# One core, chunked linear attention and a SiLU MLP: weight pieces loaded ahead of token, value and block loads, unit 2's first keys earlier, unit 3's diagonal copied by VectorE

## The chip, the cores and the metric

The kernel runs on one NeuronCore of a Trainium2 chip. The core has five engines that run side by side, each in its own program order: TensorE (PE, with its weight loads shown as PEld), VectorE (DVE), ScalarE (ACT), GpSimd (POOL) and SyncE (SP). In this kernel nearly every DMA is issued by SP, so SP's program is one long queue of transfers, and a transfer starts only when SP has come to it. The metric is device time in microseconds (us), median of several runs. The profile shows one execution, and its times are counted from the start of its span.

## The reference: what is computed

Two blocks follow each other. The first is a linear attention with a state that decays per channel, over 4 batches, 8 heads, 768 tokens and 48 channels per head:

```python
for t in range(S):
    cur = einsum('bhd,bhe->bhde', u * k[t], v[t])
    y[:, :, t] = einsum('bhd,bhde->bhe', r[t], state + cur)
    state = w[t][..., None] * state + einsum('bhd,bhe->bhde', k[t], v[t])
```

Its output, as 3072 rows of 384, goes through an MLP: `h = x @ w_in` (384 to 2048), `g = h * sigmoid(h)`, `out = g @ w_out` (2048 to 384). The two weight matrices come in 64 bits, all else in 32.

## The kernel before, in words

**Units.** The tokens are cut into six chunks of 128, and the four batches into two pairs. That makes 12 units, numbered 0 to 11; a unit is 128 tokens of two batches and all heads. "Unit 2" below is the third.

**Attention of a unit.** Decays, queries and keys (w, r, k) are turned so that channels lie on partitions (`turn`, L360; for units from 2 on by VectorE transposes at L374, out of a room `raw` that two units use in turn). The scores of a chunk are built level by level, l = 0 to 6: at level l the queries (`grow_queries`, L624, VectorE) and the keys (`grow_keys`, L630, GpSimd) are multiplied with products of decays over 2^l tokens (`product`, L419, GpSimd), matmuls make scores (`score_products`, L688, matmul at L703), and VectorE (L721) or ScalarE (L800) keeps the wanted part of them in `score`. The first keys of unit 2 are made by `odd_ones` (L657, ScalarE) and `start_keys` (L662, GpSimd, tensor_tensor at L669); `level(2, 1)` (L757) is the first to use them. The diagonal of the scores has a path of its own: products on GpSimd (`bonus`, L434, lines 448, 450 and 452), sums on VectorE (L457, L461), four small DMAs (L467) that move the sums to where tokens lie on partitions, small copies (`bonus_spread`, L581, copies at L595 and L597), and a predicated copy into `score` (`bonus_write`, L604). From unit 4 on the diagonal goes by blocks of 8 tokens instead (`block_bonus`, `block_sum`, `block_move`, `block_spread`).

**From attention to MLP.** `y_state` and `y_values` (L834, L858) make the output yt of a unit, `update` (L884) the state. `move_x` (L920) moves yt into xt with ten DMAs on SP (L928). `up(i, m)` (L995, matmul at L1000) makes one eighth of the 2048 channels: twelve matmul records, six for each half, which read xt's three column groups c = 0, 1, 2 in this order. Its result lies in one of two PSUM rooms `p_h`, which ScalarE's SiLU (L1009) frees. `down` (L1017, L1022) is the second product for unit 0; from unit 1 on it is made of seven smaller products (`quarter`, L1052, L1066), which need sums of activations (`sums`, L1042) and of weights (`weight_sums`, L1038).

**Weights.** They come as 16 pieces, 0 to 15, of 768 KB each (8 of w_in, then 8 of w_out), by `load_weight` (L202, DMA at L206), and are made into 32-bit numbers by `head_weight` and `tail_weight` (ScalarE, L223, L225, L231), `join_weight` (VectorE, L242, L243) and `add_weight` (GpSimd, L255). A piece waits for room: pieces 11 to 15 may be loaded when pieces 5, 8, 9, 10 and 11 are joined, and `join_weight` issues those loads at its end.

**Order.** No scheduler orders the work: each call appends its instructions to the engines' programs, so the order of calls in `do(...)` is the order in each engine's queue. The first part, up to unit 2, is written out by hand (L1107 to L1163): lists `others[m]` stand between the weight pieces, and lists of block loads (`block_loads`, L949: sixteen DMAs of `load_blocks`, L114 and L123, for each of w, k and r of a unit) are dealt out among them. From unit 3 on a loop (L1165) lays each unit's groups from `mix(i)` (L954 on) between the steps of the MLP: the seven quarters of unit i-2, then the eight ups of unit i-1. In `mix`, the line `loads = ...` (L981) says which block loads a unit issues, and these are dealt out over its later groups. `move_x(3)` is in the second group of `mix(4)`, so on SP it stands behind all loads that `mix(3)` issues; `up(3, 0)` needs it. `move_x(2)` stands in the hand-written part, and `up(2, 0)` needs it.

## Time and profile before

| | |
|---|---|
| median of 3 runs | 598.62 us (598.1 to 599.99) |
| the profiled execution | 599.11 us, of which its span is 597.3 us |
| TensorE busy, matmuls | 587.5 us, 98% of the span |
| VectorE, ScalarE, GpSimd busy | 411.6, 232.7, 351.5 us |
| granted TensorE clock | 1.00 |
| chain that ended last | PE 82%, DVE 5%, POOL 4%, ACT 2%, SP's queue 2%, DMA 2% |

How to read it: busy time of an engine is the union of its instructions. A line of the timeline gives start and duration in us, engine (SPq is SP issuing a DMA), the line of the kernel, the operation, what is written and read, a count of merged instructions, and in brackets the idle time before it with what ended it. A DMA line of SP is the time of issuing it; its landing comes later (median 1.9 us for the xt transfers, 2.2 us for 32 KB of w, 6.4 us for a 768 KB piece of w_out, by the page's DMA part).

### The profile page before, as it was taken

Reading aid. Unit: us, or ns where it says so; the run is one execution under the profiler, and the core shown is the slowest. Engines: PE = TensorE matmul, PEld = TensorE weight load, DVE = VectorE, ACT = ScalarE, POOL = GpSimd, SP = SyncE. Lnnn points to the kernel's source line nnn. Section 1 sums busy time; section 2 is a strip of 40 time slices with the busy share of each in tenths; the row PEclk is TensorE's granted clock in tenths of the full one; section 3 lists DMA queues with packets and bytes.
Section 4 is the critical chain, followed back from the end, with each engine's and each line's share of the span. In section 5 each row is a group of like instructions: output and inputs, shape, how many; then the busy total and the mean of one; then the engine's idle time right before and its main releaser. Section 6 shows DMA issues by size and latency. Waiting matters only on the chain.

```text
span 597.3 us, 14760 instructions
## 1 busy us (share of the span) xinstructions
PE 587.5 (98%) x5790; PEld 527.8 (88%) x5790; DVE 411.6 (69%) x709; ACT 232.7 (39%) x516; POOL 351.5 (59%) x414
## 2 busy tenths in 40 slices
PE   8999999999999999999999999999999999999997
PEld 7787866699899899899899899889889889889997
DVE  7879788798596695596696696686587587542041
ACT  6788874531530540440350351361351251250110
POOL 5998768447578568278378477477477567500000
PEclk9999999999999999999999999999999999999999
DMA  9965794443542543543543643643543531101000
GB/s 227 301 148 149 157 283 75 59 76 51 126 61 66 106 66 52 129 69 53 130 67 55 138 62 52 130 65 52 120 75 52 113 63 27 36 1 28 28 0 27
DMA packets 203078, 53.42 MB, mean 89 GB/s; under 512 B 186752, under 2 KB 194816, under 8 KB 203008
## 3 DMA queue, kind: packets, MB, share of 16 engines
q1 hardware_dynamic: 201424, 51.88, 42.7%
q8 instruction: 46, 0.75, 0.6%
q10 hardware_dynamic: 1584, 0.59, 0.5%
q14 instruction: 24, 0.20, 0.1%
HBM read 43.21 MB, written 5.24 MB: 81 GB/s over the span
## 4 chain that ended last, share of the span: by engine, by line
PE 82%; DVE 5%; POOL 4%; ACT 2%; SPq 2%; DMA 2%; issue 2%; POOLq 0%; DVEq 0%; ACTq 0%
PE p_h L1000 35%; PE p_o L1066 34%; PE p_m L1022 3%; PE p_m L864 2%; PE p_sc L703 2%; PE p_m L843 2%; SPq L123 2%; PE p_m L703 1%; DVE score L721 1%; POOL w_out_sb L255 1%; PE p_sc L892 1%; PE p_sc L819 1%; DMA own<-in_moe_w_out_dram 1%; DMA raw<-in_r_dram 1%; DVE score L604 1%
## 5 line engine op out<-in xcount | busy, mean ns | idle before, releaser
L1000 PE MATMUL p_h<-xt,w_in_sb 128*128 128x256 f32 x1152 | 259.8, 383 | 1.6 <-POOL tk L669 0.7
L1000 PEld LDWEIGHTS p_h<-xt,w_in_sb 128*128 128x128 f32 x1152 | 215.5, 190 | 33.3 <-ACT gt L1009 1.3
L1009 ACT ACTIVATE gt<-p_h 128x512 f32<-128x512 f32 x90 | 53.5, 595 | 172.5 <-PE p_h L1000 172.2
L645 POOL TENSOR_TENSOR tk<-tk,tw 128x256 f32<-128x256 f32 x128 | 93.9, 755 | 35.4 <-issue 21.0
L507 POOL TENSOR_TENSOR ruk<-tokens_rk 128x768 f32<-128x768 f32 (+1 forms) x32 | 51.4, 1616 | 64.4 <-DMA tokens_rk<-in_k_dram 34.6
L1066 PE MATMUL p_o<-own,temps 128*128 128x192 f32 x528 | 87.9, 326 | 0.0
L1066 PE MATMUL p_o<-w_out_sb,gt 128*128 128x192 f32 x508 | 86.4, 326 | 0.0
L1066 PEld LDWEIGHTS p_o<-own,temps 128*128 128x128 f32 x528 | 86.1, 190 | 0.1
L1066 PEld LDWEIGHTS p_o<-w_out_sb,gt 128*128 128x128 f32 x508 | 83.4, 190 | 0.6
L1048 DVE TENSOR_TENSOR temps<-gt 128x256 f32<-128x256 f32 x84 | 50.3, 599 | 25.7 <-ACT gt L1009 25.3
L627 DVE TENSOR_TENSOR tr<-tr,tw 128x512 f32<-128x512 f32 x61 | 54.1, 887 | 14.7 <-PE p_m L703 11.2
L422 POOL TENSOR_TENSOR tw<-tw 128x256 f32<-128x256 f32 (+6 forms) x83 | 40.4, 487 | 35.4 <-DVE tw L374 31.5
L615 ACT COPY tk<-tk 128x256 f32<-128x256 f32 x52 | 21.0, 403 | 102.6 <-POOL tk L645 80.1
L721 DVE COPY_PREDICATED score<-mask,p_sc 128x512 f32<-128x512 int8 x42 | 31.1, 796 | 3.2 <-PE p_sc L703 3.0
L1075 DVE TENSOR_TENSOR partial<-p_o,partial 128x192 f32<-128x192 f32 x33 | 11.7, 355 | 27.8 <-PE p_o L1066 27.8
L1066 PE MATMUL p_o<-w_out_sb,temps 128*128 128x192 f32 x176 | 30.4, 326 | 0.0
L1048 DVE TENSOR_TENSOR temps<-temps,gt 128x256 f32<-128x256 f32 x43 | 29.1, 677 | 1.5
L1075 DVE TENSOR_TENSOR temps<-p_o,partial 128x192 f32<-128x192 f32 x22 | 7.9, 358 | 31.5 <-PE p_o L1066 25.3
L541 DVE TENSOR_REDUCE block_sums<-ruk 128x4 f32<-128x192 f32 (+1 forms) x48 | 24.2, 545 | 7.1 <-POOL ruk L507 7.1
L1066 PEld LDWEIGHTS p_o<-w_out_sb,temps 128*128 128x128 f32 x176 | 28.9, 190 | 0.0
L869 ACT COPY yt<-p_m 48x512 f32<-48x512 f32 x40 | 23.2, 581 | 13.9 <-PE p_m L864 13.1
L703 PEld LDWEIGHTS p_sc<-tr,tk 48*64 48x64 f32 x960 | 17.3, 134 | 12.1 <-issue 7.7
(188 smaller groups left out, 814.2 us busy)
## 6 DMA issues: line engine op xcount, KB each, us to landing
w_out_sb<-in_moe_w_in_dram SPq DMA_DIRECT2D x6, 768.0 KB, 7.6
w_out_sb<-in_moe_w_out_dram SPq DMA_DIRECT2D x4, 768.0 KB, 6.4
own<-in_moe_w_out_dram SPq DMA_DIRECT2D x4, 768.0 KB, 6.1
tokens_rk<-in_r_dram SPq DMA_DIRECT2D x8, 384.0 KB, 4.5
tokens_rk<-in_k_dram SPq DMA_DIRECT2D x8, 384.0 KB, 5.4
tokens_w<-in_w_dram SPq DMA_DIRECT2D x8, 384.0 KB, 6.4
xt<-yt SPq DMA_DIRECT2D x60, 48.0 KB, 1.9
raw<-in_w_dram SPq DMA_DIRECT2D x80, 32.0 KB, 2.2
```

Of the source, the lines that this page charges most:

```text
L422: engine.tensor_tensor(out=up, in0=t[:, :, 0::2], in1=t[:, :, 1::2], op=ALU.mult)
L507: mul = lambda out, one, two: nc.gpsimd.tensor_tensor(out=out, in0=one, in1=two, op=ALU.mult)
L541: add = lambda out, have: nc.vector.tensor_reduce(out=out, in_=have, axis=mybir.AxisListType.X, op=ALU.add)
L627: nc.vector.tensor_tensor(out=odd, in0=odd, in1=tw[i][l][:, :, 0::2][:, :, :, None].to_broadcast([128, Q, L >> (l + 1), c]), op=ALU.mult)
L645: nc.gpsimd.tensor_tensor(out=out, in0=have, in1=odd_products(i, l, b, *blocks), op=ALU.mult)
L703: nc.tensor.matmul(to, lhsT=tk[i][rows, X[l % 2] + p, x * 64:(x + 1) * 64], rhs=have, start=True, stop=True)
L721: nc.vector.copy_predicated(out=dst, mask=masks[l][:, :, None].to_broadcast([128, NB, NP, ni, c]), data=sc[e].rearrange("p (b q) (i c) -> ...
L869: nc.scalar.copy(out=yt[i][PD * e:PD * e + D, x::2, :, :], in_=p_yt[i, e][PD * x:PD * x + D].rearrange("p (q b) t -> p q b t", b=NB))
L1000: nc.tensor.matmul(p_h[:, a, :], lhsT=w_in_sb[:, c, f * 128:(f + 1) * 128], rhs=xt[i][:, c, :], start=(c == 0), stop=(c == KC - 1))
L1009: nc.scalar.activation(out=gt[i, m], in_=p_h, func=AF.Silu)
L1048: nc.vector.tensor_tensor(out=out, in0=one, in1=two, op=op)
L1066: nc.tensor.matmul(p, lhsT=left(f), rhs=right[:, f, :], start=(f == 0), stop=(f == FH - 1))
```

## The change

It has four parts, all in the order of calls or in the engine of one step.

1. `bonus_spread` copies with VectorE instead of ScalarE for units above 2, that is for unit 3 alone.
2. In `mix`, the r blocks of unit i+1 are issued in unit i already for i = 3 (before: from i = 4 on). So r of unit 4 is issued in `mix(3)`; the hand-written part now loads only w and k of unit 4.
3. In the hand-written part, the r blocks of unit 2 go behind piece 11, the values of unit 2 and the tokens of unit 3 (`load_values(2)`, `load_rk(3)`) behind pieces 14 and 15, and the blocks of unit 3 one to two places later.
4. For unit 2, `odd_ones`, the first `start_keys` and the products are called earlier, `reverse_v(2)` and `weight_sums(0)` later.

```diff
@@ bonus_spread
-        nc.scalar.copy(out=both_b[:, 0], in_=diag[i][0])
+        copy = nc.vector.tensor_copy if i > NTOK else nc.scalar.copy
+        copy(out=both_b[:, 0], in_=diag[i][0])
         for g in range(4):
-            nc.scalar.copy(out=both_b[(3 - g) * 32:(4 - g) * 32, 1], in_=diag[i][1][g * 32:(g + 1) * 32])
+            copy(out=both_b[(3 - g) * 32:(4 - g) * 32, 1], in_=diag[i][1][g * 32:(g + 1) * 32])
@@ mix
-        loads = [*at(i >= NPAIR and ahead, *block_loads(i + 1, "r")), *at(i + NSLOT < len(units), *block_loads(i + NSLOT, "wk"))]
+        loads = [*at(i >= NPAIR - 1 and ahead, *block_loads(i + 1, "r")), *at(i + NSLOT < len(units), *block_loads(i + NSLOT, "wk"))]
@@ pieces 4 to 6
-    others = {1: [(bonus_sum, 1, 0), (bonus_sum, 1, 1), (load_rk, 2), *blocks[8:12]], 2: [*both(update, 0)],
-              3: [(bonus_spread, 1), (reverse_v, 1), (clear, 1), (load_values, 2)]}
+    others = {1: [(bonus_sum, 1, 0), (bonus_sum, 1, 1), (load_rk, 2)], 2: [*both(update, 0), *blocks[8:10]],
+              3: [(bonus_spread, 1), (reverse_v, 1), (clear, 1), *blocks[10:12]]}
@@ after piece 9
-  ... (bonus_sum, 2, 1), (load_rk, 3), (up, 1, 0), *both(turn, 2, "w"))
+  ... (bonus_sum, 2, 1), (up, 1, 0), *both(turn, 2, "w"))
@@ pieces 10 to 15
-    others = {0: [(up, 1, 1), (down, 0, 0, 0), *both(turn, 2, "k"), (product, 2, 0), (product, 2, 1)],
-              1: [(up, 1, 2), *both(turn, 2, "r"), *[(product, 2, l) for l in range(2, NL)], *blocks[0:3]],
-              2: [(down, 0, 0, 1), (odd_ones, 2), (start_keys, 2, nc.gpsimd, True), (grow_queries, 2, 0), *blocks[3:6]],
-              3: [(up, 1, 3), (start_keys, 2, nc.gpsimd, False), (reverse_v, 2), *blocks[6:9]], 4: [(level, 2, 1), (up, 1, 4), *blocks[9:12]],
-              5: [(down, 0, 0, 2), (up, 1, 5), (weight_sums, 0)]}
+    others = {0: [(up, 1, 1), (down, 0, 0, 0), *both(turn, 2, "k"), (odd_ones, 2), (product, 2, 0), (product, 2, 1)],
+              1: [(up, 1, 2), *both(turn, 2, "r"), (start_keys, 2, nc.gpsimd, True), *[(product, 2, l) for l in range(2, NL)], (load_values, 2)],
+              2: [(down, 0, 0, 1), (grow_queries, 2, 0), (load_rk, 3), *blocks[0:2]],
+              3: [(up, 1, 3), (start_keys, 2, nc.gpsimd, False), *blocks[2:5]], 4: [(level, 2, 1), (up, 1, 4), *blocks[5:8]],
+              5: [(down, 0, 0, 2), (up, 1, 5), *blocks[8:12]]}
@@ behind the pieces
-    blocks = block_loads(4)
+    blocks = block_loads(4, "wk")
-  ... (down, 0, 1, 1), (sums, 1, 0))
+  ... (down, 0, 1, 1), (sums, 1, 0), (weight_sums, 0))
-  ... (prepare, 2, 5), (down, 0, 1, 2),
+  ... (prepare, 2, 5), (reverse_v, 2), (down, 0, 1, 2),
```

TensorE's instructions and their order are the same in both kernels. SP issues the same 667 entries in another order.

More of the change, by code (lines that the diff above doesn't have):

```diff
@@ L1141 @@
        (tail_weight, 9), (turn_k, 1), (dense_x, 1, 0), (head_weight, 9, [0]), (dense_x, 1, 1), (head_weight, 9, [1]),
-       (join_weight, 9), (add_weight,), (tail_weight, 10), (head_weight, 10), *both(update, 1), (bonus_sum, 2, 1), (load_rk, 3), (up, 1, 0), *both(turn, 2, "w"))
+       (join_weight, 9), (add_weight,), (tail_weight, 10), (head_weight, 10), *both(update, 1), (bonus_sum, 2, 1), (up, 1, 0), *both(turn, 2, "w"))
     blocks = block_loads(3)
-    others = {0: [(up, 1, 1), (down, 0, 0, 0), *both(turn, 2, "k"), (product, 2, 0), (product, 2, 1)],
-              1: [(up, 1, 2), *both(turn, 2, "r"), *[(product, 2, l) for l in range(2, NL)], *blocks[0:3]],
-              2: [(down, 0, 0, 1), (odd_ones, 2), (start_keys, 2, nc.gpsimd, True), (grow_queries, 2, 0), *blocks[3:6]],
-              3: [(up, 1, 3), (start_keys, 2, nc.gpsimd, False), (reverse_v, 2), *blocks[6:9]], 4: [(level, 2, 1), (up, 1, 4), *blocks[9:12]],
-              5: [(down, 0, 0, 2), (up, 1, 5), (weight_sums, 0)]}
+    others = {0: [(up, 1, 1), (down, 0, 0, 0), *both(turn, 2, "k"), (odd_ones, 2), (product, 2, 0), (product, 2, 1)],
[3 more added lines that the diff above has]
+              5: [(down, 0, 0, 2), (up, 1, 5), *blocks[8:12]]}
     for m in range(6):
@@ L1153 @@
     second.append(ctx.enter_context(tc.tile_pool(name="po", bufs=1, space=bass.MemoryType.PSUM)))
-    blocks = block_loads(4)
-    do(*blocks[0:2], (level, 2, 2), (prepare, 2, 3), (down, 0, 1, 0), (down, 0, 0, 3), (down, 0, 1, 1), (sums, 1, 0))
-    do(blocks[2], (burst, 2, 3), (keep_level, 2, 3), (keep_level, 2, 4), (go_on, 2, 4), (prepare, 2, 5), (down, 0, 1, 2),
+    blocks = block_loads(4, "wk")
+    do(*blocks[0:2], (level, 2, 2), (prepare, 2, 3), (down, 0, 1, 0), (down, 0, 0, 3), (down, 0, 1, 1), (sums, 1, 0), (weight_sums, 0))
+    do(blocks[2], (burst, 2, 3), (keep_level, 2, 3), (keep_level, 2, 4), (go_on, 2, 4), (prepare, 2, 5), (reverse_v, 2), (down, 0, 1, 2),
        (bonus_spread, 2), (sums, 1, 1), *blocks[3:7], (down, 0, 1, 3))
```

## Prediction

> **What bounds the kernel now.** I read the page first: TensorE is busy 98% of the span, at a granted clock of 1.00, and the chain that ended last lies on it for 82%. What a change can give is therefore TensorE's idle time, and what it can cost is new idle time there. So the second view was TensorE's waits, the third its timeline.

> ```profile
> PE 587.5 (98%) x5790; PEld 527.8 (88%) x5790; DVE 411.6 (69%) x709; ACT 232.7 (39%) x516; POOL 351.5 (59%) x414
> ...
> PEclk9999999999999999999999999999999999999999
> ```

> ```profile
> PE p_sc L703 <- POOL tk L669: 1.5, 1, 1.5
> ...
> PE p_h L1000 <- ACT gt L1009: 0.6, 1, 0.6
> ```

> ```profile
> 89.92 0.70 PE L703 MATMUL p_sc<-tr,tk 48*64 48x64 f32 x32 [1.48 <-POOL tk L669]
> ...
> 158.03 8.39 PE L1000 MATMUL p_h<-xt,w_in_sb 128*128 128x256 f32 x36 [0.63 <-ACT gt L1009]
> ...
> 192.51 13.22 PE L1000 MATMUL p_h<-xt,w_in_sb 128*128 128x256 f32 x60
> ...
> 238.29 13.37 PE L1000 MATMUL p_h<-xt,w_in_sb 128*128 128x256 f32 x60
> ```

> The reader sees two stalls that the change can touch: 1.48 us before level 1 of unit 2, which waits for its first keys, and 0.63 us at 157.4, where a room p_h is not yet freed by ScalarE. From 166 to the tail no idle is listed. The last two lines are `up(3, 0)` and `up(4, 0)` with what follows; the second takes 0.15 us more for as many matmuls. The fourth view is SP's queue:

> ```profile
> 142.72 9.22 SPq L123 DMA_DIRECT2D raw<-in_r_dram  x16
> ...
> 153.01 2.45 SPq L467 DMA_DIRECT2D diag<-own_sums  x4
> ...
> 158.96 11.30 SPq L123 DMA_DIRECT2D raw<-in_w_dram  x16
> ...
> 173.90 7.84 SPq L123 DMA_DIRECT2D raw<-in_k_dram  x16
> 181.85 6.35 SPq L928 DMA_DIRECT2D xt<-yt  x10
> ```

> From 153.01 to 188.2 SP issues without a pause, and xt of unit 3 is last in that row. This queue is what decides the change.

> **Part 1: the stall at 89.9, gain 1.48 us.** GpSimd's first-key pair (L669, 1.30 us) ran at 88.57, behind the add of piece 12 (L255, 86.46, 2.15 us), which waited for VectorE, which waited for ScalarE's tail of piece 12, whose head waited 1.34 us for its DMA (81.55). After the change the pair stands behind the add of piece 11 and two products. Pieces: load 11 is issued near 60.0 instead of 71.42, so head 11 loses its wait of 0.65 us; loads 12 and 13 near 72.7 instead of 76.06 (they land after about 5.5 us as before, so near 78, and head 12 wants its piece at 80.1); load 14 is ready when piece 10 is joined, near 78.2, and lands near 83.7, where head 14 waited until 89.51. GpSimd: add of piece 10 at 78.33 as now, two products to 81.84, add 11 to 83.7, the key pair to 85.0. TensorE arrives at 88.44, the end of `up(1, 3)`, so 3.4 us are to spare. The grown queries (L627, now 86.24 to 86.93) come near 85.5. I take the whole 1.48. What is late next: level 2 needs keys at 97.0 instead of 98.5; they (L645, now until 98.08) end near 95.5, because piece 14 comes 3 us earlier. The second level burst has `weight_sums(0)` (L1040, 1.75 us) put ahead of its keeps; the next queries are then done near 111.8, with TensorE there at 112.7. Thin, but cover. If a product or add slips by 3.4 us, the gain shrinks from there on; bounds 0 to 1.48.

> The loads moved past the pieces all have later readers: r of unit 2 lands near 75 (its transpose L374 runs at 81.68), the values of unit 2 near 86 (reversed near 112), tokens of unit 3 near 92 (first product L448 at 141.78). SP then comes to the block loads of unit 3 near 88 instead of 85.71, but meets landed pieces: before, this row of ten issues took 7.7 us, since the two own pieces of 84.58 held it. I cost that at nothing; if SP were 3 us late by `move_x(2)` (132.83), `up(2, 0)` would begin to wait, and no sooner.

> **Part 2: the stall at 157.4, gain 0.78 us, but hidden.** ScalarE stood in front of its copies L595 and L597 for the diagonal's DMA (until 156.64), with two SiLUs queued behind; a second wait of about 0.15 us came at 163.4 (the SiLU at 162.91 stood behind ScalarE's eight plus four keeps, L800). With the copies on VectorE the SiLUs run when their matmuls end. VectorE waits there for the same DMA anyway, at its shuffle L598; it now makes five copies. The trace has no such copy on VectorE; the nearest rows are the shuffle of 128x16 (0.17 us) and a cast of 128x2 (0.54 us), so five cost 0.9 to 2.7 us against 1.04 us on ScalarE; I take 0.9, the shuffle being as wide. Behind them stand L604 (2.5 us) and the keeps. Up to 0.78 us is won, or nothing by the upper end. It does not matter, for the next part takes it back.

> **Part 3: xt of unit 3, the cost.** SP's program now holds r of unit 4 behind the diagonal's DMAs. Before, those sixteen were issued at 142.72 to 151.94, while SP had nothing better: the diagonal's sums (L461) ended at 152.23. Now SP idles there and issues them later, ahead of w, values and k of the next units and of the ten xt transfers.
> - The sixteen issues cost 16 x 0.494 = 7.9 us (k at 173.90: 7.84 for sixteen). Their row now takes 9.22, because its last issue took 1.82 us, beside a packet of the instruction queue at 150.28. By its place in the program such a pause falls into the wait that SP has there anyway for the token loads: the w row takes 11.30 instead of 7.84, most of it this. Bounds 0 to 1.4 us, I take 0.15.
> - The diagonal's DMAs can go at 152.26 instead of 153.01 (two output stores stood behind the r row): minus 0.75. They also come 1.48 us earlier with TensorE.
> - So the last xt transfer is issued at 187.6 + 7.9 + 0.15 - 0.75 - 1.48 = 193.4 and lands 1.9 later, at 195.3. In other words the row of r, w, values and k, 53 issues, starts at 156.75 (the diagonal at 150.8 and 5.95 us on, as from 153.01 to 158.96 now) and takes 31 us; the like row of unit 4, from 199.81 to 231.55, took 31.7.
> - `up(3, 0)` reads the last column group with its fifth matmul record, 0.88 us after its start (12 take 2.69). Before, that was at 192.51 + 0.88 = 193.39, with the data there since 189.5: cover 3.9 us. `up(4, 0)` shows the rule at work: start 238.29, need 239.17, last issue 237.2 plus 1.9.
> - New: 195.3 against 193.39, that is 1.9 us later than before, although TensorE could have been there 2.26 us earlier. A stall of about 4.2 us eats both gains and 1.9 more.
> - The 0.15 us of `up(4, 0)` go: SP gets through unit 4's loads as before, TensorE arrives later. Minus 0.15.

> **Sum:** +1.9 - 0.15 = +1.75; of the pause I had taken nearly the lower end, so I forecast a little more, +1.9. From then on TensorE is dense, so it stays. On the profiled execution's 599.11 us that is 601.0; it is 0.49 above the median of the three runs, so I forecast 598.62 + 1.9 = 600.5. A difference of about 0.3%, 1.8 us, is what a measurement can tell from none.

> [...] The trace's row: an issue of 32 KB occupies SP for 0.45 us and the next starts 0.494 later, fifty-three fill 31 us. [...] Second row: idle gaps of up to 1.48 us left the granted clock at 1.00; no run here shows 4 us. [...]

> **The rivals.**
> - *The queue keeps up, faster.* If the 53 issues took 26.2 us (0.494 each, no waits or pauses), xt would land near 190.5 and the need is at 191.1: both gains stay, 598.62 - 2.26 = 596.3. For it: 53 x 0.494; the later part of the row runs so. Against it: every such row in the trace has the token wait and pauses, and unit 4's took 31.7. The stall begins where the row takes more than 26.7 us, and each us above costs one; from 28.9 on the kernel is slower than before. 0.13.
> - *Worse, the front gain doesn't come.* First keys or a level behind them wait for another thing, or `weight_sums(0)` is in the way; then the diagonal is not earlier either and xt lands 1.48 later: +3.3, 601.9. Against it: 3.4 us to spare. 0.12.
> - *Worse, the row is longer.* A pause of 1.1 to 1.4 us falls into the ten xt issues (at 138.88 one took 1.70), or the restart after the gap costs as much: +3.0 to +3.3, near 601.8. Against: the xt rows of units 3 and 4 hold none (issues of at most 0.60 us). 0.15.
> - *Forecast:* xt late by what is worked out, +0.5 to +3.0. 0.60.

> **Numbers.** The forecast's 0.60 lies about 0.33 above +1.8 and 0.27 within. Slower by over 0.3%: 0.33 + 0.12 + 0.15 = 0.60; within: 0.27; faster: 0.13. The range leaves out the fast rival and the edges: 598.8 to 602.6, which takes in the unknown costs.

> **What would show it.** In the changed profile: no idle before L703 near 88.4, and its key pair L669 near 84; head loads of pieces without DMA waits but for small ones; no wait for L1009 near 156; SP with nothing to issue near 145 to 150, then r, w, values and k in a row of 30 to 32 us; xt issued from about 187.5; TensorE waiting for xt 4 us in all at `up(3, 0)`, near 190 to 195. I am wrong if xt's DMAs are issued by 183, or if TensorE waits at another place.

## The result and the profile after

The changed kernel took 603.14 us (median of 6 runs, 602.65 to 604.44), the kernel before 599.66 us beside it (6 runs, 598.1 to 600.73). The ratio is 1.0063, 95% interval 1.0045 to 1.0082: slower by 3.5 us, where +1.9 us was forecast and 602.6 was the upper end of the range. The profiled execution of the changed kernel took 602.65 us, with a span of 600.8 us (before: 599.11 and 597.3). From `bonus_spread` on (L595) the lines carry numbers one higher than before: L1000 is now L1001, L703 is L704, L669 is L670, L928 is L929, and ScalarE's SiLU is L1010. By the profiles SP issues 750 DMAs in either kernel, and not the 667 entries named above.

The page of the changed kernel: the engines' busy times, and the granted clock in the 40 slices.

```profile
PE 590.1 (98%) x5790; PEld 529.6 (88%) x5790; DVE 407.8 (68%) x714; ACT 231.7 (39%) x511; POOL 352.0 (59%) x414
...
PEclk9999999999999899999999999999999999999999
```

TensorE has as many instructions as before and is busy 2.6 us longer, and one slice of the clock row, the fourteenth (195 to 210 us), shows 8 where before there was none. A wait alone would have lengthened the span and not the busy time. The two waits that the change aimed at are gone from the view of waits; its longest group is new:

```profile
PE p_h L1001 <- DMA xt<-yt: 2.9, 2, 1.9
```

TensorE's timeline at the places shown of before:

```profile
88.55 0.70 PE L704 MATMUL p_sc<-tr,tk 48*64 48x64 f32 x32
...
155.96 8.04 PE L1001 MATMUL p_h<-xt,w_in_sb 128*128 128x256 f32 x36
...
190.09 0.70 PE L1001 MATMUL p_h<-xt,w_in_sb 128*128 128x256 f32 x2
...
192.70 1.19 PE L1001 MATMUL p_h<-xt,w_in_sb 128*128 128x256 f32 x2 [1.91 <-DMA xt<-yt]
...
194.88 14.47 PE L1001 MATMUL p_h<-xt,w_in_sb 128*128 128x256 f32 x56 [0.99 <-DMA xt<-yt]
...
241.91 13.22 PE L1001 MATMUL p_h<-xt,w_in_sb 128*128 128x256 f32 x60
```

Level 1 of unit 2 starts without idle time, and so do the 36 records (one per matmul in the trace) at 155.96. TensorE reaches `up(3, 0)` at 190.09, which is 2.42 us earlier than before. Then it waits twice for xt, before the second and before the third column group, and reads the third at 194.88, where before it was at 193.39: 1.49 us later. The 56 records from there take 14.47 us. At `up(4, 0)` it is 3.62 us behind the kernel before (241.91 against 238.29), and the 0.15 us that this one lost itself are gone (13.22 against 13.37): 3.47, which is the difference of the spans.

SP's queue in the changed kernel:

```profile
144.85 0.38 SPq L1080 DMA_DIRECT2D out_dram<-temps  x1
150.43 2.45 SPq L467 DMA_DIRECT2D diag<-own_sums  x4
...
156.38 10.17 SPq L123 DMA_DIRECT2D raw<-in_r_dram  x16
166.60 5.00 SPq L123 DMA_DIRECT2D raw<-in_w_dram  x8
...
178.21 7.85 SPq L123 DMA_DIRECT2D raw<-in_k_dram  x16
186.17 7.16 SPq L929 DMA_DIRECT2D xt<-yt  x10
```

SP has nothing to issue from 145.2 to 150.4, then the diagonal, the token loads, and r, w, values and k in a row from 156.38 to 186.06, that is 29.7 us. Last come the ten xt transfers, until 193.3.

The windows view of the changed kernel behind the wait. Its columns are window, length, busy time and instructions of PE, PEld, DVE, ACT and POOL, granted clock, DMA share, GB/s:

```profile
195.00:197.00 2.00, 2.00 (x5) 1.64 (x6) 0.78 (x3) 0.00 (x0) 0.00 (x0) 0.50 0.40 131
197.00:199.00 2.00, 2.00 (x6) 1.55 (x6) 0.00 (x0) 0.34 (x1) 0.00 (x0) 0.50 0.71 47
199.00:201.00 2.00, 2.00 (x11) 1.72 (x10) 0.00 (x0) 0.56 (x2) 1.20 (x2) 0.94 0.82 212
```

This is the second part of the loss. From 195 to 199 TensorE never idles, and yet it gets through 11 matmul records in 4 us, as many as in the 2 us from 199 on. The granted clock is 0.50. By the trace's record of the clock it fell to 0.50 at 192.40 and rose at 199.22, so it was low for 6.82 us. The matmuls ran in it from 194.88 to 199.22, 4.34 us, and lost half of that, 2.2 us.

**The theory** to be tested, A: the change costs 1.5 us because xt of unit 3 comes late, behind r of unit 4 on SP, and 2.1 us more because the clock falls in that wait. **The rivals**, B: the 56 records are slow for another reason (loads, PSUM, DMA traffic), so that a busy TensorE would not mend it; and C: the loss is in the front part or in the copies, and the order of r(4) alone is harmless.

### The profile page after: what moved, and what is told of

It reads as the page before. It is cut to its first block, busy times and chain, and to the rows that moved or that the text cites. A ratio compares the mean times of both kernels' runs of the same rounds, so it can differ in the third digit from the quotient of the medians.

```text
span 600.8 us, 14760 instructions
## 1 busy us (share of the span) xinstructions
PE 590.1 (98%) x5790; PEld 529.6 (88%) x5790; DVE 407.8 (68%) x714; ACT 231.7 (39%) x511; POOL 352.0 (59%) x414
## 4 chain that ended last, share of the span: by engine, by line
PE 81%; POOL 5%; DVE 5%; SPq 3%; DMA 3%; issue 2%; ACT 1%; DVEq 0%; POOLq 0%; ACTq 0%
PE p_h L1001 37%; PE p_o L1067 30%; PE p_m L1023 4%; PE p_sc L704 2%; PE p_m L865 2%; POOL tk L646 2%; SPq L123 2%; PE p_m L844 2%; PE p_m L704 1%; POOL w_in_sb L255 1%; DMA u_bc<-in_u_dram 1%; SPq L929 1%; DMA raw<-in_r_dram 1%; DVE score L722 1%; PE p_sc L893 1%
## 5 line engine op out<-in xcount | busy, mean ns | idle before, releaser
L1001 PE MATMUL p_h<-xt,w_in_sb 128*128 128x256 f32 x1152 | 262.6, 385 | 3.8 <-DMA xt<-yt 2.9
L1001 PEld LDWEIGHTS p_h<-xt,w_in_sb 128*128 128x128 f32 x1152 | 217.3, 191 | 36.4 <-DMA xt<-yt 2.3
L1010 ACT ACTIVATE gt<-p_h 128x512 f32<-128x512 f32 x90 | 53.7, 596 | 188.2 <-PE p_h L1001 187.9
L646 POOL TENSOR_TENSOR tk<-tk,tw 128x256 f32<-128x256 f32 x128 | 93.2, 749 | 45.9 <-issue 28.0
L628 DVE TENSOR_TENSOR tr<-tr,tw 128x512 f32<-128x512 f32 x61 | 55.6, 912 | 15.7 <-PE p_m L704 12.5
L1049 DVE TENSOR_TENSOR temps<-gt 128x256 f32<-128x256 f32 x84 | 46.2, 550 | 27.7 <-ACT gt L1010 27.4
L1076 DVE TENSOR_TENSOR temps<-p_o,partial 128x192 f32<-128x192 f32 x22 | 7.9, 358 | 32.4 <-PE p_o L1067 26.2
L1067 PEld LDWEIGHTS p_o<-w_out_sb,temps 128*128 128x128 f32 x176 | 28.9, 190 | 0.0
L655 POOL TENSOR_TENSOR tk<-tk,tw 128x256 f32<-128x256 f32 x32 | 28.0, 894 | 0.0
L1049 DVE TENSOR_TENSOR temps<-temps,gt 128x256 f32<-128x256 f32 x43 | 26.5, 615 | 1.5
```

The costliest lines, as they stand in the source:

```text
L628: nc.vector.tensor_tensor(out=odd, in0=odd, in1=tw[i][l][:, :, 0::2][:, :, :, None].to_broadcast([128, Q, L >> (l + 1), c]), op=ALU.mult)
L646: nc.gpsimd.tensor_tensor(out=out, in0=have, in1=odd_products(i, l, b, *blocks), op=ALU.mult)
L655: nc.gpsimd.tensor_tensor(out=have, in0=have, in1=odd_products(i, l, b, [2, NP * ni]), op=ALU.mult)
L1001: nc.tensor.matmul(p_h[:, a, :], lhsT=w_in_sb[:, c, f * 128:(f + 1) * 128], rhs=xt[i][:, c, :], start=(c == 0), stop=(c == KC - 1))
L1010: nc.scalar.activation(out=gt[i, m], in_=p_h, func=AF.Silu)
L1049: nc.vector.tensor_tensor(out=out, in0=one, in1=two, op=op)
```

## The experiments

The first four kernels ran on one chip, beside 29 runs of the kernel before (median 598.75 us). The other four ran on a second chip, beside 31 runs of it (median 599.04 us). Parts are counted as in the list of the change: 1 the copies, 2 r of unit 4, 3 and 4 the front.

**e1: the gap filled.** Thirty transposes of the identity, into a room that nobody reads, stand ahead of `up(3, 0)`. They add work on TensorE; nothing is left out.

```diff
+    def fill(n):
+        p = ps.tile([128, 2, TU], F32, name="p_h", bufs=2)
+        for x in range(n):
+            nc.tensor.transpose(p[:, 0, 0:L], ident, ident)
...
         steps = downs(i - 2) + ups(i - 1)
+        if i == NPAIR:
+            steps[7].insert(0, (fill, 30))
```

> The changed kernel with 30 transposes of the identity (about 0.12 us each, 3.6 us, into a p_h room that nobody reads) on TensorE just ahead of up(3, 0); nothing else differs. Theory A, two terms: xt comes late (1.5 us) and the granted clock then stands at 0.50 from 192.4 to 199.2 (2.1 us). With the gap filled the clock stays at 1.00, the third column group still starts near 194.9, and the kernel is 1.4 us slower than before (ratio 1.002) instead of 3.5. Rival B, the long matmuls behind 194.9 are not the clock's doing but come from the traffic or VectorE there: it stays 3.5 us slower (1.006).

Measured: 600.69 us (12 runs, 600.12 to 601.25), ratio 1.0029 [1.0012, 1.0046], with a granted clock of 0.999 to 1.00 in every run. TensorE's timeline of this kernel:

```profile
190.26 3.49 PE L1108 MATMUL p_h<-ident 128*128 128x128 f32 x30
193.59 1.03 PE L1001 MATMUL p_h<-xt,w_in_sb 128*128 128x256 f32 x4
195.14 12.32 PE L1001 MATMUL p_h<-xt,w_in_sb 128*128 128x256 f32 x56 [0.52 <-DMA xt<-yt]
```

xt is no earlier (the third column group is read at 195.14, in the changed kernel at 194.88), but the same 56 records take 12.32 us instead of 14.47. So 2.15 us were the clock. B falls: the loads and the DMA traffic are the same here. What is left of the loss is the late xt.

**e2: r of unit 4 alone.** The kernel before with nothing but part 2 of the change.

```diff
-        loads = [*at(i >= NPAIR and ahead, *block_loads(i + 1, "r")), *at(i + NSLOT < len(units), *block_loads(i + NSLOT, "wk"))]
+        loads = [*at(i >= NPAIR - 1 and ahead, *block_loads(i + 1, "r")), *at(i + NSLOT < len(units), *block_loads(i + NSLOT, "wk"))]
-    blocks = block_loads(4)
+    blocks = block_loads(4, "wk")
```

> The kernel before with the r loads of unit 4 moved into mix(3), nothing else of the change. Theory A: the xt transfers of unit 3 are issued 7.9 - 0.75 us later and land near 196.6, where the third column group is wanted at 193.4: 3.2 us, and with a gap of this size the clock falls for about 7 us, 2.1 more: 5.3 us slower (1.009); 3.2 (1.005) if the clock stays. Rival B, this part frees the diagonal and xt is late only because the first part let TensorE arrive sooner: no slower than before, or 0.5 us faster.

Measured: 603.92 us (6 runs, 602.28 to 604.41), ratio 1.0074 [1.0045, 1.0102]. The timeline of this kernel:

```profile
193.13 0.95 PE L1000 MATMUL p_h<-xt,w_in_sb 128*128 128x256 f32 x2 [1.56 <-DMA xt<-yt]
195.29 14.75 PE L1000 MATMUL p_h<-xt,w_in_sb 128*128 128x256 f32 x56 [1.22 <-DMA xt<-yt]
```

The same two waits, the same slow row (the clock was 0.50 from 193.38 to 200.20), the whole of the loss. C falls: part 2 is not harmless, by itself it costs what the whole change costs. TensorE comes to `up(3, 0)` at 190.87 here, 1.64 us earlier than before. Of this, 0.59 us is there already at level 1 of unit 2 (89.33 against 89.92), which this kernel does not change: its stall was 0.43 us in this execution and not 1.48. The other 1.05 us comes on the way, where the wait at 157.4 is gone; the diagonal's DMAs go at 151.22 instead of 153.01.

**e3: all but r of unit 4.** The changed kernel with part 2 taken back.

```diff
-        loads = [*at(i >= NPAIR - 1 and ahead, *block_loads(i + 1, "r")), *at(i + NSLOT < len(units), *block_loads(i + NSLOT, "wk"))]
+        loads = [*at(i >= NPAIR and ahead, *block_loads(i + 1, "r")), *at(i + NSLOT < len(units), *block_loads(i + NSLOT, "wk"))]
-    blocks = block_loads(4, "wk")
+    blocks = block_loads(4)
```

> The changed kernel with the r loads of unit 4 back in the hand-written part, all else as changed. Theory A: xt of unit 3 is in time, no gap at up(3, 0). But the front part leaves SP about 1.5 us later at these r loads, so the diagonal's DMAs of unit 3 start near 154.7 while TensorE comes 1.4 us earlier, and up(2, 6) waits about 3.5 us for its room p_h: 1 us slower than before (1.002), 3 us if the clock falls in that gap. Rival B, the r loads are the only harm: both gains stay, 2.3 us faster (0.996).

Measured: 602.52 us (12 runs, 599.72 to 604.16), ratio 1.0048 [1.0025, 1.0072]. The gain of the front part does not come back. TensorE's timeline, then SP's, of this kernel:

```profile
156.83 5.45 PE L1001 MATMUL p_h<-xt,w_in_sb 128*128 128x256 f32 x24
165.16 5.49 PE L1001 MATMUL p_h<-xt,w_in_sb 128*128 128x256 f32 x12 [2.89 <-ACT gt L1010]
```

```profile
145.06 8.59 SPq L123 DMA_DIRECT2D raw<-in_r_dram  x16
...
154.71 2.46 SPq L467 DMA_DIRECT2D diag<-own_sums  x4
```

With sixteen r issues in their old place, SP comes to the diagonal at 154.71, in the kernel before at 153.01: its queue runs later, since `move_x(2)` starts at 135.71 instead of 132.83. So with the order of part 3 SP is 2.9 us late at `move_x(2)` and 1.7 us at the diagonal, in this pair of executions, and I had costed that at nothing. VectorE gets the diagonal late, ScalarE's keeps of `score` (L801) wait behind VectorE's predicated copy until 160.74, two SiLUs stand behind them, and TensorE waits 2.89 us for a room. The clock fell here too, from 164.47 to 171.29: 12 records took 5.49 us, where 24 had taken 5.45. The mean clock divides the runs: 599.7 to 600.7 us in the three at 0.999 to 1.00, about 604 in the four at 0.993 or 0.994. So one and the same order of work may lose the clock or keep it.

**e7: the front part alone.** The same, with ScalarE's copies as well: parts 3 and 4 of the change by themselves.

```diff
-        copy = nc.vector.tensor_copy if i > NTOK else nc.scalar.copy
+        copy = nc.scalar.copy
```

> The changed kernel with the r loads of unit 4 back in the hand-written part and the diagonal's copies back on ScalarE: what is left is the earlier pieces and first keys. Theory A: the idle before level 1 of unit 2 is gone (1.4 us), but the diagonal of unit 3 comes about 1.7 us later, and ScalarE, standing before its copies, holds two SiLUs: TensorE waits some 3.5 us near 156 to 162, in two parts, 1 us slower than before in all, 3 us if the clock falls in the wait. Rival B, the front part's gain stays: 1.4 us faster (0.9977).

Measured: 602.65 us (8 runs, 600.54 to 605.63), ratio 1.0061 [1.0037, 1.0085]. The timeline of this kernel:

```profile
159.43 9.71 PE L1001 MATMUL p_h<-xt,w_in_sb 128*128 128x256 f32 x36 [2.74 <-ACT gt L1010]
```

The same place, one ScalarE step earlier: the two SiLUs stand behind the copies that wait for the diagonal, which is issued at 154.40. The clock was 0.50 from 159.44 to 162.85, 3.41 us, and 36 records took 9.71 us where the changed kernel needs 8.04. So the front part by itself makes the kernel slower, and the reading that its gain stays when nothing else is changed falls. It is a loss at another place than the changed kernel's. Part 2, which brings the loss at unit 3's xt, is also what lets the diagonal go at 150.43 and takes this one away.

**e5: the copies alone.** The kernel before with VectorE's copies for unit 3.

```diff
-        nc.scalar.copy(out=both_b[:, 0], in_=diag[i][0])
+        copy = nc.vector.tensor_copy if i > NTOK else nc.scalar.copy
+        copy(out=both_b[:, 0], in_=diag[i][0])
```

> The kernel before with the five small copies of unit 3's diagonal on VectorE instead of ScalarE, nothing else of the change. Theory A: the SiLUs no longer stand behind the diagonal's DMA and the idle of 0.63 us at 157.4 goes, but the second wait, for the room of up(2, 6), is set by the diagonal itself, which comes when it came: 0 to 0.3 us faster, that is the same (1.000). Rival B, the idle at 157.4 is won whole: 0.8 us faster (0.9987), the idle after it not grown.

Measured: 599.06 us (11 runs, 598.29 to 599.89), ratio 0.9991 [0.9977, 1.0005]. The timeline:

```profile
156.77 5.45 PE L1001 MATMUL p_h<-xt,w_in_sb 128*128 128x256 f32 x24
163.26 2.86 PE L1001 MATMUL p_h<-xt,w_in_sb 128*128 128x256 f32 x12 [1.04 <-ACT gt L1010]
```

The wait of 0.63 us at 157.4 has gone, and one of 1.04 us at 162 has come: the SiLUs behind ScalarE's keeps are next in line. The keeps wait until 158.82 for VectorE's predicated copy, and VectorE until 156.45 for the diagonal's DMAs. The row of 12 takes 2.86 us, so the clock stayed. The copies are worth nothing as long as the diagonal itself is no earlier.

**e4: k of unit 5 behind xt.** If SP's row is too long, sixteen of its issues should go behind `move_x(3)`.

```diff
-        loads = [*at(i >= NPAIR - 1 and ahead, *block_loads(i + 1, "r")), *at(i + NSLOT < len(units), *block_loads(i + NSLOT, "wk"))]
+        loads = [*at(i >= NPAIR - 1 and ahead, *block_loads(i + 1, "r")), *at(i + NSLOT < len(units), *block_loads(i + NSLOT, "w" if i == NPAIR - 1 else "wk"))]
...
-                       *bonus_steps(i, 4, 5), (move_x, i - 1)],
+                       *bonus_steps(i, 4, 5), (move_x, i - 1),
+                       *at(i == NPAIR, *block_loads(i + 1, "k"))],
```

> The changed kernel with the sixteen k loads of unit 5 taken from ahead of the xt transfers of unit 3 to behind them, where SP waits anyway. Theory A: xt is issued from about 178.3 and landed by 186.5, TensorE does not wait at up(3, 0), the clock stays at 1.00, and both gains stay (2.3 us faster, 0.996), less up to 0.9 us if xt of unit 4 (lands near 237.5, wanted near 236.8) becomes the next wait: 1.4 to 2.3 us faster. Rival B, the diagonal on VectorE or the reordered front part costs time of its own: not faster than before.

Measured: 599.80 us (12 runs, 597.76 to 602.95), ratio 1.0014 [0.9993, 1.0035]: the loss is gone, the expected gain is not there. SP's queue and TensorE's timeline of this kernel:

```profile
178.96 6.33 SPq L929 DMA_DIRECT2D xt<-yt  x10
185.34 8.85 SPq L123 DMA_DIRECT2D raw<-in_k_dram  x16
...
195.25 0.39 SPq L560 DMA_DIRECT2D kept<-block_sums  x1
```

```profile
190.42 13.22 PE L1002 MATMUL p_h<-xt,w_in_sb 128*128 128x256 f32 x60
...
237.55 0.70 PE L1002 MATMUL p_h<-xt,w_in_sb 128*128 128x256 f32 x2 [0.64 <-DMA xt<-yt]
...
239.77 12.32 PE L1002 MATMUL p_h<-xt,w_in_sb 128*128 128x256 f32 x56 [1.52 <-DMA xt<-yt]
```

`up(3, 0)` starts at 190.42 without a wait, 2.09 us before the kernel before. But SP issues k until 194.2 and comes to unit 4's own diagonal (L560) at 195.25, no earlier than in the kernel before (195.20); all of unit 4's loads follow that, and at `up(4, 0)` the gain goes back in waits of 2.2 us. The queue was emptied at one place and not shortened. The clock did not fall in the profiled execution, although one gap was 1.52 us: the 56 records took 12.32. In four of the twelve runs it did, by their mean clocks of 0.994 and 0.997 (600.65 to 602.95 us).

**e6: k of unit 5 on ScalarE's queue.** The same sixteen transfers, issued by ScalarE, four in each of the first four groups of `mix(4)`.

```diff
-    def load_blocks(i, name, g):
+    def load_blocks(i, name, g, queue=nc.sync):
...
-                nc.sync.dma_start(out=room[(2 * e + a) * 32:(2 * e + a + 1) * 32, :, g, 0:d1 - d0],
+                queue.dma_start(out=room[(2 * e + a) * 32:(2 * e + a + 1) * 32, :, g, 0:d1 - d0],
...
-        loads = [*at(i >= NPAIR - 1 and ahead, *block_loads(i + 1, "r")), *at(i + NSLOT < len(units), *block_loads(i + NSLOT, "wk"))]
+        loads = [*at(i >= NPAIR - 1 and ahead, *block_loads(i + 1, "r")), *at(i + NSLOT < len(units), *block_loads(i + NSLOT, "w" if i == NPAIR - 1 else "wk"))]
+        if i == NPAIR:
+            for g in range(4):
+                groups[g].append((load_blocks, i + 1, "k", g, nc.scalar))
```

> The changed kernel with the sixteen k loads of unit 5 issued by ScalarE, four in each of the first four groups of unit 4, instead of by SP. Theory A: SP's issuing is the bound, so taking sixteen issues off it lets xt of unit 3 land by 187 and leaves SP free for the block sums of unit 4 at about 193, so that xt of unit 4 lands near 237.0, where it is wanted near 236.8: 2 us faster than before (0.9967), 1.4 if ScalarE's issues (0.45 us each) hold a copy that TensorE needs. Rival B, the number of transfers in flight is the bound, not who issues them: up(4, 0) waits 2 us as in the run before, no faster than before.

Measured: 598.07 us (11 runs, 597.05 to 599.19), ratio 0.9983 [0.9971, 0.9994]. This beats both kernels: it is 1.0 us below the one before, where the changed one is 3.5 above it. SP's queue, then TensorE's timeline:

```profile
179.50 6.33 SPq L929 DMA_DIRECT2D xt<-yt  x10
...
193.85 0.33 SPq L560 DMA_DIRECT2D kept<-block_sums  x1
...
229.84 6.28 SPq L929 DMA_DIRECT2D xt<-yt  x10
```

```profile
191.16 13.22 PE L1004 MATMUL p_h<-xt,w_in_sb 128*128 128x256 f32 x60
...
236.94 13.22 PE L1004 MATMUL p_h<-xt,w_in_sb 128*128 128x256 f32 x60
```

Both xt transfers come in time and neither up waits. So SP's issuing is the bound that the change runs into, and it is lifted without touching a byte of what is moved. The sixteen k issues had taken 7.85 us of SP's queue in the changed kernel (from 178.21), and in this case that time decides, by a ratio to the kernel before of 0.9983 against 1.0063.

I had expected 2 us below the kernel before and measured 1.0. In the profiled execution `up(4, 0)` is 1.35 us earlier than before and TensorE's last row 1.5 us, but the span is only 1.0 us shorter: 0.5 us goes in the tail behind that row. Nor was the front's share 1.48 us in every execution. With the front as before, level 1 of unit 2 starts at 89.92, 89.33 (e2) and 89.36 (e5), behind stalls of 1.48, 0.43 and 0.40 us; with the changed front it starts at 88.55 to 89.42 in the seven profiles, here at 89.16. By the means of these, the front brings about 0.5 us. What spreads them by 0.6 to 0.9 us is open.

**e8: twelve transposes instead of thirty.** Is it the length of one gap that makes the clock fall, or how much of a stretch is idle?

```diff
-            steps[7].insert(0, (fill, 30))
+            steps[7].insert(0, (fill, 12))
```

> As the run with 30 transposes ahead of up(3, 0), but 12 (1.4 us): two gaps of about 0.8 and 1.7 us are left, no longer than the 1.48 us that left the clock alone before, or little longer. If the fall of the clock goes by the longest gap or by the idle share of some 3.4 us, it stays at 1.00 and the kernel is 1.4 us slower than before (1.002 to 1.003); if it falls all the same, 3.5 us (1.006).

Measured: 600.82 us (10 runs, 599.89 to 602.38), ratio 1.0030 [1.0016, 1.0044]. The clock was 1.00 in nine of the ten runs and 0.997 in the one of 602.38 us.

```profile
190.60 1.53 PE L1108 MATMUL p_h<-ident 128*128 128x128 f32 x12
...
193.18 0.67 PE L1001 MATMUL p_h<-xt,w_in_sb 128*128 128x256 f32 x2 [0.62 <-DMA xt<-yt]
...
195.34 12.32 PE L1001 MATMUL p_h<-xt,w_in_sb 128*128 128x256 f32 x56 [1.49 <-DMA xt<-yt]
```

1.5 us of work at the start of the wait does what 3.5 us did. The gaps that are left, 0.62 and 1.49 us, left the clock up in the profiled execution. The run does not decide between one long gap and the idle share; the times at which the clock fell do, in the last section.

## Why the prediction was wrong, step by step

- **The stall at 89.9: the mechanism right, the 1.48 us that of one execution.** The first keys' pair ran at 83.78 (forecast 84), level 1 at 88.55 without idle time (88.4). Loads 12 and 13 were issued from 75.14 and not near 72.7, but landed at 79.65 and 81.68, before ScalarE came to them at 80.27 and 83.98. That the two profiles differ here by 1.37 us is in part luck: in e2 and e5, with the front of before, the stall was 0.43 and 0.40 us.
- **Its loads on SP "at nothing": right in the sum, wrong by itself.** `move_x(2)` began at 134.66 in the changed kernel, 1.83 us later than before. Only because r of unit 4 is gone from 142 on does this vanish in SP's idle time; without the change's part 2 (e3, e7) it becomes a wait of 2.7 to 2.9 us for unit 3's diagonal. The forecast had looked only at `up(2, 0)` as the place where a late SP would show.
- **The stall at 157.4: right.** VectorE's copies took 0.16 and 0.70 us, 0.86 in all (0.9 was taken), and the wait is gone. The gain goes in the wait for xt, as forecast. Without the earlier diagonal there would have been none: e5, the copies alone, has 0.9991 [0.9977, 1.0005].
- **xt of unit 3: right, a little too dear.** The diagonal went at 150.43 (150.8), the row started at 156.38 (156.75) and took 29.7 us (31), xt was issued from 186.17 (187.5). The ten took 7.16 us instead of 6.35, because one of them, at 189.38, took 1.41 us: the pause that the rival "the row is longer" had named. Third column group at 194.88 (195.3): 1.49 us later than before, where 1.9 was taken.
- **The step that failed** is the clock. The sum has no term for it, and it was the larger one: 2.15 us (14.47 against 12.32 in e1). The wait I had forecast rightly: the third column group is read 3.9 us later than TensorE could have read it (194.88 against 190.09 + 0.88), where 4.2 stood, and 2.9 us of that is idle. I had seen no clock below 1.00 in the profile of before, but none of its gaps was above 1.48 us, so it could not speak for this one. What was unknown should have been bounded from both sides, from 0 to what a long matmul row loses at a lower clock (2.15 us here), and the upper end taken into the range. In the trace of the changed kernel the clock fell to 0.50 at 192.40, inside the first wait, when TensorE had been idle for 1.61 us.
- **The sum:** 1.49 + 2.15 - 0.15 = 3.49 us, and the spans differ by 3.5.
- **The rivals:** that the queue keeps up fell (xt issued from 186.17, not by 183). That the front gain doesn't come is not what happened: level 1 came early and the diagonal went at 150.43. The rival with a longer row, or with a restart that costs as much, had the place right: the pause in the xt issues was there, paid for by a shorter row, and the restart cost 2.15 us and not the 1.1 to 1.4 that stood there.

## What to carry to other kernels

Where one engine issues nearly all transfers, count its issues between two deadlines (here 53 issues and ten of xt before `up(3, 0)`): moving a load later on that queue moves everything behind it (xt of unit 3 was issued from 181.85 before and from 186.17 after), and the better remedy here was another issuing engine (e6, 0.9983) and not another place in the same queue (e4, 1.0014). A gain at the front of such a chain is only kept if every later deadline has cover, that is time to spare; otherwise it comes back as a wait at the next one, as in e3 (2.89 us), e4 (2.16) and e7 (2.74). A stall on a dense TensorE of the size seen here (in these profiles the clock fell with 1.56 to 2.73 us of idle time in a window of the table below, and stayed with up to 1.48 and once with 1.63) is costed twice, once as idle time and once for the clock, the second as a range from 0 (2.15 us in the changed kernel); where it could not be avoided, thirty or twelve transposes into an unread room ahead of it saved the second part (600.69 us in e1 and 600.82 in e8, against 603.14). And a stall read from one profile may be that execution's: here 1.48 us in one, 0.4 in two others.

## What the runs showed of the hardware that I had not expected

The clock fell in waits that were short: two gaps of 1.91 and 0.99 us in the changed kernel, 1.56 and 1.22 in e2. The second gap had no part in it. The clock fell at 192.40 and 193.38, before the second gap began (193.89 and 194.08). It did not fall with 0.62 and 1.49 us (e8) in nine runs of ten, nor with 0.64 and 1.52 in the profiled execution of e4.

```profile
188.99:192.40 3.41, 1.80 (x67) 1.32 (x66) 3.01 (x5) 0.00 (x0) 2.78 (x3) 1.00 0.17 43
192.40:195.81 3.41, 2.12 (x4) 1.34 (x5) 3.34 (x7) 0.00 (x0) 0.00 (x0) 0.50 0.53 172
```

| profile | window, us | TensorE idle in it, us | clock after it |
|---|---|---|---|
| changed kernel | 188.99 to 192.40 | 1.61 | falls |
| e2 | 189.96 to 193.37 | 1.56 | falls |
| e3 | 161.05 to 164.47 | 2.19 | falls |
| e7 | 156.02 to 159.44 | 2.73 | falls |
| before | 87.16 to 90.57 | 1.48 | stays |
| e4 | 235.05 to 238.46, 238.46 to 241.87 | 0.86, 1.31 | stays |
| e8 | 190.88 to 194.29, 194.29 to 197.70 | 1.05, 1.05 | stays |
| e5 | 159.96 to 163.37 | 1.04 | stays |
| before, tail | 592.33 to 595.75 | 1.63 | stays |

So in these profiles the fall goes with what a window holds. A gap that a window's edge divides can go free (e4, 1.52 us) where an undivided one of nearly the same length does not (e2, 1.56 us). The clock rises after a window without idle time (all four) and not after one with 0.69 to 1.29 us of it. By the mean clocks of its runs (0.994, 0.997, 1.00), e3 had two low windows, one or none, and 7 of the 60 runs of the kernel before, at 0.996 or 0.997, had about one. That the grid falls differently from run to run, and that this is why, fits but is not shown. Nor is idle time all that counts: the last line kept the clock with 1.63 us, where 1.56 and 1.61 lost it in windows with 64 small matmuls. Where the limit lies is open.
